# A retention-then-mixer kernel on one core: a plan that counts TensorE's instruction blocks, two-token loads for two head pairs only, and q cast into column order

## The chip, the cores and the metric

The kernel runs on 1 core of one Trainium2 chip. The metric is device time in microseconds (us) of one execution, the median over runs. Engines are named as in the profile: PE is the matmul engine (PEld its weight loads), DVE the vector engine, ACT the scalar engine, POOL and SP two engines that mostly issue DMA transfers here.

## What is computed

```python
def _attn_ref(q, k, v):                       # q, k, v: (4, 8, 768, 64) f32
    gamma = 1.0 - 2.0 ** (-5.0 - np.arange(H))
    state = np.zeros((B, H, D, D))
    for t in range(S):
        state = gamma[None, :, None, None] * state + np.einsum('bhd,bhe->bhde', k[:, :, t], v[:, :, t])
        y[:, :, t] = scale * np.einsum('bhd,bhde->bhe', q[:, :, t], state)
...
def _moe_ref(x, w_tok1, w_tok2, w_ch1, w_ch2):   # x: (4, 768, 512)
    xt = x.transpose(0, 2, 1)
    h = np.maximum(xt @ w_tok1, 0.0) @ w_tok2    # 768 -> 256 -> 768, over tokens
    u = x + h.transpose(0, 2, 1)
    h2 = np.maximum(u @ w_ch1, 0.0) @ w_ch2      # 512 -> 1536 -> 512, over channels
    return u + h2
```

The first function's output (batch, head, token, 64) is laid out as (batch, token, 512) and is the second one's x.

## The kernel before, in words

The work is cut into 16 pairs of heads (4 batches of 4 pairs, a pair's two heads side by side in 128 partitions) and 6 chunks of 128 tokens. `front(b, p)` does one pair, with matmuls in f16:

- **Load.** k, q and v come from device memory, cast to f16 on the way by POOL's queue (`load`, L489 to L517). Three loads of batch 0 are in `HARD`: they come as f32 over SP's queue, and the engines cast them.
- **Decay and transpose.** k is scaled by powers of gamma (`decayed`, L541) and transposed (`turn`, L576): on TensorE for batches 0 and 1 ("t"), by a DMA for batches 2 and 3 ("x"). q of batches 0 and 1 is loaded "wide" (a partition holds six consecutive tokens of a head) and is transposed head by head, 12 matmuls that each use a half of the array's columns ("w", L591); for batches 2 and 3 it goes like k. A HARD q is first cast to f16 (L572).
- **State and scores.** Five partial states (`st`, L618), a scan over them on DVE (L643), the scaled states `cross` (L654), the scores (`sc`, L665), their masked copy `am` on DVE (L686), then `av` and `y2` (L693 to L720), which add in-chunk and cross-chunk output in two banks.
- **Token mixing.** `t1` (L743) and `t2` (L764), which adds onto the same two banks, so that these hold u. It is copied twice, to f16 and to f32, and the f16 copy is transposed (L803 on TensorE or L792 by DMA) into `uT`.

A pair of batch 0 is **paired** before the change (`PAIRED = (0,)`): its k and v are loaded with two consecutive tokens of a head in one packet. A partition then holds neighbouring tokens, so `st`, `sc` and `av` split into half-array matmuls: 20 instead of 10, 24 instead of 12, and 24 instead of 12. Paired forms stand on L623, L675 and L698, the others on L630, L679 and L707.

`back(b)` does the channel mixing of a batch: for batch 0 a plain product (`w8`, L838: 96 matmuls of 128x384), for the others one with seven products in place of eight (L911); the second product (L1036) is of the latter kind for all. DVE adds the result to X, and SP or ACT stores it.

**What sets the order.** Every step is an `Op`. Two strings written in the file hold the order of all of them (`ORDERED`, two letters an op) and the engine of each (`WAYS`). `arrange` replays that order with a clock of its own: an op starts when its inputs, its engine and a buffer are there. It picks the buffer or bank of each op and the order in which the engines' instructions are written; within an engine that is `ORDERED`'s. Where its clock leaves TensorE free for over 400 ns in the first 21 us, filler matmuls on zeros (L1163) are put in. Before the change its clock knows engines, semaphores, buffers and DMA queues, and takes TensorE's instructions to be always at hand.

## Time and profile before

| | |
|---|---|
| time, median of 3 | 187.42 us (187.33 to 187.9) |
| the profiled execution | 187.37 us, of which the span of its instructions is 185.6 us (1.77 us lie outside) |
| granted TensorE clock | 1.000 |
| TensorE | 2216 weight loads and 2216 matmuls, 28 of the latter fillers |

The profile's page gives busy time by engine and, in 40 slices of the span, how busy each was. Its chain of work follows the last instruction back to what released it, step by step; "issue" there is time in which an engine waited for nothing that the profile shows. A group's row reads: line, engine, operation, out<-in, count, busy time, mean duration, idle time ahead of it. A row of busy time by stretch reads: stretch in us, its length, then for PE, PEld, DVE, ACT and POOL the busy us and, in brackets, the instructions that overlap the stretch; then the granted clock, the DMA engines' share and GB/s. Matmul durations overlap, since matmuls are pipelined: the time from a group's start to the next one's, which the chain shows, is what a group takes.

### The profile page before, as it was taken

How to read it: one execution, taken by the hardware profiler on the slowest of the kernel's cores; microseconds unless marked ns; L12 is line 12 of the kernel's file. 1: busy time of each engine (PE TensorE's matmuls, PEld its weight loads, DVE VectorE, ACT ScalarE, POOL GpSimd, SP SyncE). 2: the span in 40 equal slices, each digit the busy share in tenths (PEclk: the TensorE clock that was granted, in tenths of full speed). 3: DMA queues.
4: the chain of work that ended last, by engine and by line, in shares of the span. 5: the costliest groups of instructions: out<-in, count | busy, mean ns of one | idle time of the engine just before them, and what ended most of it. 6: DMA issues, size and time to landing. Idle time of an engine off the chain costs nothing.

```text
span 185.6 us, 5517 instructions
## 1 busy us (share of the span) xinstructions
PE 175.3 (94%) x2216; PEld 134.7 (73%) x2216; DVE 167.7 (90%) x431; ACT 128.5 (69%) x298; POOL 51.3 (28%) x63
## 2 busy tenths in 40 slices
PE   7688898899999999999999999999999999999992
PEld 3355787566778989876658988965778996668881
DVE  5599988878999999999999999999899999878993
ACT  3797887576899997999998474899765024654220
POOL 8964775462503906844004000000000000000000
PEclk9999999999999999999999999999999999999999
DMA  5999999999995998999999969340762114110044
GB/s 178 196 186 196 184 201 204 167 192 198 157 151 62 129 153 107 159 152 134 188 196 162 189 85 220 79 85 0 123 232 62 58 62 144 66 58 0 5 180 160
DMA packets 86106, 25.33 MB, mean 136 GB/s; under 512 B 75072, under 2 KB 83264, under 8 KB 86080
## 3 DMA queue, kind: packets, MB, share of 16 engines
q0 software_dynamic: 61808, 12.78, 82.1%
q1 hardware_dynamic: 22688, 9.70, 27.9%
q10 hardware_dynamic: 1584, 2.49, 3.7%
q8 instruction: 17, 0.28, 0.6%
q14 instruction: 9, 0.07, 0.1%
HBM read 26.74 MB, written 6.29 MB: 178 GB/s over the span
## 4 chain that ended last, share of the span: by engine, by line
PE 86%; DVE 4%; ACT 3%; DMA 3%; issue 1%; SPq 1%; DVEq 0%
PE bank L1036 30%; PE bank L911 22%; PE bank L838 8%; PE bank L743 6%; PE bank L764 5%; DMA hs<-in_q_dram 3%; PE bank L679 3%; PE bank L717 3%; PE bank L707 2%; PE bank L803 2%; PE bank L630 1%; DVE am L686 1%; PE bank L698 1%; PE bank L591 1%; DVE qT L602 1%
## 5 line engine op out<-in xcount | busy, mean ns | idle before, releaser
L686 DVE TENSOR_TENSOR am<-bank,mask 128x384 f16<-128x384 f32 x64 | 32.9, 546 | 0.7 <-PE bank L679 0.5
L864 ACT COPY us<-bank 128x384 f32<-128x384 f32 (+1 forms) x44 | 19.1, 437 | 17.8 <-PE bank L1036 11.6
L1036 PEld LDWEIGHTS <-hs 128*128 128x128 f16 x288 | 27.0, 98 | 3.1
L1036 PE MATMUL bank<-wsum,hs 128*128 128x256 f16 x216 | 27.8, 273 | 0.0
L859 ACT ACTIVATE h<-bank 128x384 f16<-128x384 f32 x50 | 23.3, 493 | 5.2 <-PE bank L838 3.5
L911 PE MATMUL bank<-hs,late 128*128 128x384 f16 x108 | 23.9, 326 | 0.0
L505 POOL DMA_DIRECT2D v<-in_v_dram x12 | 12.1, 1012 | 37.5 <-PE bank L707 13.4
L1036 PEld LDWEIGHTS <-h 128*128 128x128 f16 x216 | 20.6, 98 | 2.6
L932 DVE CUSTOM_DVE_ANT_0 h<-bank,us 128x384 f16<-128x384 f32 x36 | 19.0, 548 | 1.4 <-ACT us L864 0.7
L1050 DVE TENSOR_TENSOR X<-X,bank 128x256 f32<-128x256 f32 x48 | 19.2, 411 | 0.5 <-PE bank L1036 0.3
L1036 PE MATMUL bank<-wc,h 128*128 128x256 f16 x144 | 19.5, 273 | 0.0
L911 PEld LDWEIGHTS <-late 128*128 128x128 f16 x144 | 13.4, 98 | 7.9 <-DVE hs L883 0.2
L838 PE MATMUL bank<-uT,wc 128*128 128x384 f16 x96 | 17.7, 326 | 0.6 <-DVE X L729 0.6
L643 DVE SCALAR_TENSOR_TENSOR U<-U,gp,bank 128x64 f32<-128x64 f32 x64 | 15.9, 273 | 0.7
L911 PE MATMUL bank<-uT,wc 128*128 128x384 f16 x72 | 16.3, 326 | 0.0
L729 ACT COPY X<-bank 128x384 f32<-128x384 f32 x31 | 14.7, 493 | 2.2 <-PE bank L764 2.0
L729 ACT CAST x<-bank 128x384 f16<-128x384 f32 x27 | 12.2, 479 | 4.4 <-PE bank L717 4.2
L764 PE MATMUL bank<-h,wt 128*128 128x128 f16 x192 | 15.2, 219 | 0.0
L864 ACT COPY bank<-bank 128x384 f32<-128x384 f32 (+1 forms) x27 | 11.7, 436 | 4.9 <-PE bank L911 2.4
L729 ACT CAST u<-bank 128x384 f16<-128x384 f32 x25 | 11.8, 494 | 4.4 <-PE bank L764 4.2
L654 ACT ACTIVATE cross<-U,gp 64x320 f16<-64x320 f32 x25 | 13.8, 557 | 1.0 <-DVE U L643 0.7
L911 PEld LDWEIGHTS <-wc 128*128 128x128 f16 x108 | 9.9, 98 | 5.4
(98 smaller groups left out, 347.0 us busy)
## 6 DMA issues: line engine op xcount, KB each, us to landing
out_dram<-X SPq DMA_DIRECT2D x14, 256.0 KB, 2.4
v<-in_v_dram POOLq DMA_DIRECT2D x16, 192.0 KB, 8.0
k<-in_k_dram POOLq DMA_DIRECT2D x15, 192.0 KB, 9.0
q<-in_q_dram POOLq DMA_DIRECT2D x14, 192.0 KB, 9.7
wc<-in_moe_w_ch_dram POOLq DMA_DIRECT2D x5, 512.0 KB, 13.3
out_dram<-X ACTq DMA_DIRECT2D x8, 256.0 KB, 2.1
hs<-in_q_dram SPq DMA_DIRECT2D x2, 384.0 KB, 5.0
wc<-in_moe_w_ch_dram POOLq DMA_DIRECT2D x2, 256.0 KB, 8.6
```

The costliest lines, as they stand in the source:

```text
L643: nc.vector.scalar_tensor_tensor(out=u[:, c], in0=u[:, c - 1], scalar=gp[:, p:p + 1], in1=st, op0=ALU.mult, op1=ALU.add)
L654: nc.scalar.activation(r, u, AF.Copy, scale=g)
L686: nc.vector.tensor_tensor(am, SC[g].tile[:, :m * P].rearrange("p (i t) -> p i t", t=P), (mask2[:, g // 2:g // 2 + 1] if paired else mask). ...
L729: (nc.scalar.copy if e == "ACT" else nc.vector.tensor_copy)(tile(), t)
L764: nc.tensor.matmul(Y[j].tile[:, 2 * i * D:2 * (i + 1) * D], wt2[:, jt, t], H1.tile[:, jt], start=False, stop=(jt == NJ - 1), skip_group_ch ...
L838: nc.tensor.matmul(acc[:, :SH], wc1[:, ct, ft * P:(ft + 1) * P], UT.tile[:, ct, sh * SH:(sh + 1) * SH], start=(ct == 0), stop=(ct == NP - 1))
L859: nc.scalar.activation(out, src, AF.Relu)
L864: (nc.scalar.copy if e == "ACT" else nc.vector.tensor_copy)(out, src)
L911: nc.tensor.matmul(acc[:, :SH], left(ct), r[:, ct], start=first and ct == 0, stop=ct == C2 - 1, skip_group_check=True)
L932: nc.vector._custom_dve(TENSOR_ADD_SAT, out=h(m, sh), in0=R.tile[:, :SH], in1=KS.tile[:, j], s0=BIG, s1=0.0)
L1036: nc.tensor.matmul(acc[:, lo], l[:, j], r[:, j], start=first and j == 0, stop=j == K2 - 1, skip_group_check=True)
L1050: nc.vector.tensor_tensor(dst(), dst(), b_(), ALU.add)
```

## The change

It does four things.

1. **The planner's clock counts TensorE's instructions.** Each TensorE op gets a count (`ins`, two per matmul). Of every 256 instructions the plan notes when the block after next is asked for (`ASKED`) and when the first instruction of a block is needed (`NEEDED`); if it is needed earlier than `FETCH` after it was asked for, the op takes that much longer in the plan. Fillers are counted too, and their number is now set inside the plan. None of this is an instruction of its own.
2. **`PAIRED` holds two pairs of batch 0 in place of all four.** k and v of the third and fourth pair come in one-token packets, and their `st`, `sc` and `av` are the unpaired forms.
3. **A HARD q is cast into column order** (chunk, head, channel in place of head, chunk, channel), so that its transposition is 6 matmuls over the whole array, as for k, in place of 12 on half arrays. This holds for q of the first two pairs of batch 0.
4. **`ORDERED` and `WAYS` are new**, and some of the planner's DMA numbers (`OPENING`, `SOFT`, `HARD`, `PL`, `PT`).

```diff
-    PL = (1470, 1700, 2600)
-    PT = (4500, 25000)
+    PL = (1600, 2400, 2600)
+    PT = (13500, 25000)
...
+FILL, F_NS, F_COLD = 0.7, 165, 240
+BLOCK, ASKED, NEEDED, PE_0 = 256, -80, 192, 2
+FETCH = (7600, 5000, 95000)
...
+                o.fill = int((s_ - pe_at) * FILL / (F_NS if pe_at > 2000 else F_COLD)) if s_ < F_ON and s_ - pe_at > 400 else 0
+                count += 2 * o.fill
+                o.busy = way[1]
+                for x in range(count, count + o.ins):
+                    if (x - ASKED) % BLOCK == 0:
+                        fetched[(x - ASKED) // BLOCK] = s_ + (x - count) * o.busy / o.ins + FETCH[s_ > FETCH[2]]
+                    if (x - NEEDED) % BLOCK == 0 and x > NEEDED:
+                        late = fetched.get((x - NEEDED) // BLOCK, 0) - (s_ + (x - count) * o.busy / o.ins)
+                        o.busy += max(0, late)
+                count += o.ins
...
 ORDERED = (
-    "0u0a0t030v010c0x090f020m0C0d0b0e0j0w0h0r050o040l0y0g0n0s0A1x1y1z1A0F1E0q1B0p281C1F1D2f062g0B291O2a2b1S2c0E2P"
+    "0t0q000a0u0r010d0v030l0C0c0j0b0w0s02090e0x0m1x050A061E0f0o0y0h0p0i1F040z1y1z0n1A1B280g1C0B1D2f2g1O0E2N1S1G1Q"
...
-    PAIRED = (0,)
+    PAIRED = {(0, 0), (0, 1)}
...
-            elif b in PAIRED:
+            elif (b, p) in PAIRED:
...
-                d = tile_of(QF, [P, 2, NC, D], F16)
+                d = tile_of(QF, [P, NC, 2, D], F16).rearrange("p c h d -> p h c d")
                 (nc.scalar.copy if e == "ACT" else nc.vector.tensor_copy)(d, QH.tile)
...
+            split = mode == "w" and (b, p, "q") not in HARD
...
-                    if mode == "w":
+                    if split:
                         for j in range(2):
                             nc.tensor.transpose(tp[rows_of(j), c * P:(c + 1) * P], src.tile[:, j, c], ident16)
                     else:
                         nc.tensor.transpose(tp[:, c * P:(c + 1) * P], src.tile[:, c].rearrange("p h d -> p (h d)"),
                                             ident16)
```

TensorE has 4434 instructions in its order before (with two that are no matmuls or weight loads) and 4288 after it; 28 fillers become 35.

Three places show what the new order does. First POOL's queue, from its first load to v of the fourth pair. In a name, the letter is the tensor and the first number the buffer; 128x6x128 is a two-token load of k or v, 128x12x64 a one-token load, wt1 and wt2 are the token weights. Before:

```order
L501 DMA k0_102<-in_k_dram 128x6x128
L497 DMA q0_118<-in_q_dram 128x2x384
L501 DMA v0_127<-in_v_dram 128x6x128
L501 DMA k1_138<-in_k_dram 128x6x128
L501 DMA v1_144<-in_v_dram 128x6x128
L481 DMA wt2_85<-in_moe_w_tok2_dram 128x2x384
L501 DMA v2_215<-in_v_dram 128x6x128
L481 DMA wt1_84<-in_moe_w_tok1_dram 128x6x256
L497 DMA q3_338<-in_q_dram 128x2x384
L501 DMA k2_350<-in_k_dram 128x6x128
L501 DMA v3_392<-in_v_dram 128x6x128
```

The same queue after the change, as far as v of the fourth pair:

```order
L514 DMA q0_108<-in_q_dram 128x2x384
L518 DMA v0_114<-in_v_dram 128x6x128
L518 DMA k0_129<-in_k_dram 128x6x128
L518 DMA v1_136<-in_v_dram 128x6x128
L522 DMA k1_162<-in_k_dram 128x12x64
L522 DMA k2_171<-in_k_dram 128x12x64
L522 DMA v2_199<-in_v_dram 128x12x64
L498 DMA wt1_84<-in_moe_w_tok1_dram 128x6x256
L514 DMA q3_280<-in_q_dram 128x2x384
L498 DMA wt2_85<-in_moe_w_tok2_dram 128x2x384 x2
L522 DMA v3_356<-in_v_dram 128x12x64
```

Before, the second half of wt2 stands between wt1 and q3 (a row that reads like the first half's and isn't shown again). The twelve loads are the same; the last k has moved from behind wt1 to ahead of it, both halves of wt2 have moved behind q3, and four loads (two k, two v) have become one-token loads, three of them ahead of wt1.

Second, TensorE from the first t1 product on, one matmul of each group. Before (L743 is t1, L698 av, L717 y2, L764 t2, L591 a transposition of q, L623 st, L593 a transposition of k):

```order
L743 MATMUL bank5_508<-x160_474,wt1_84 128x128
...
L698 MATMUL bank6_528<-v1_144,am5_352 128x64
...
L764 MATMUL bank1_441<-h10_554,wt2_85 128x128
...
L591 MATMUL bank5_575<-ident16_74,q3_338 64x128
...
L743 MATMUL bank4_602<-x161_573,wt1_84 128x128
...
L698 MATMUL bank3_618<-v2_215,am2_505 128x64
...
L623 MATMUL bank7_649<-v3_392,k160_598 64x64
...
L593 MATMUL bank4_692<-ident16_74,k160_598 128x128
```

And after (L761 is t1, L609 a transposition of q, L716 a paired av, L725 an unpaired one, L782 t2, L648 an unpaired st, L821 a transposition of u):

```order
L761 MATMUL bank6_492<-x160_461,wt1_84 128x128
...
L609 MATMUL bank0_513<-ident16_74,q3_280 64x128
...
L716 MATMUL bank1_529<-v1_136,am6_434 128x64
...
L725 MATMUL bank2_558<-v2_199,am3_527 128x64
...
L782 MATMUL bank4_408<-h10_555,wt2_85 128x128
...
L761 MATMUL bank7_606<-x161_587,wt1_84 128x128
...
L648 MATMUL bank0_624<-v3_356,k160_358 64x64
...
L821 MATMUL bank4_637<-ident16_74,u160_604 128x128
```

The fourth pair's q is now transposed directly behind the first t1, ahead of the second pair's av; the third pair's av has moved ahead of the first t2; and the fourth pair's k is no longer transposed here (that now stands ahead of the first t1).

Third, DVE at the second q. Before (L459 and L458 are constants, L602 writes a transposed q, L686 is am):

```order
L572 CAST q1_146<-hs0_94 128x768
L549 TENSOR_SCALAR k160_148<-us0_90,gk2_78 128x3x64
L459 MEMSET cross0_81 128x320
L458 TENSOR_SCALAR mask_75<-away_66 128x128
L602 TENSOR_TENSOR qT0_194<-bank0_169,X0_123 128x768
L427 TENSOR_SCALAR lgs_67<-lgr_79,away_66 128x8
L602 TENSOR_TENSOR qT1_213<-bank2_199,X0_123 128x768
L686 TENSOR_TENSOR am0_249<-bank6_222,mask2_77 128x384
```

After (L589 is the cast, L620 the transposed q, L566 a decayed k, L704 am):

```order
L620 TENSOR_TENSOR qT0_168<-bank0_151,X0_127 128x768
L566 TENSOR_SCALAR k160_173<-us1_96,gk2_78 128x3x64
L472 MEMSET gp_73 64x1
L473 MEMSET gp_73 64x1
L589 CAST q2_180<-hs1_102 128x2x6x64
L620 TENSOR_TENSOR qT1_210<-bank2_203,X0_127 128x768
L704 TENSOR_TENSOR am0_254<-bank6_215,mask2_77 128x384
```

The cast of the second pair's q has moved from ACT to DVE, and it writes 128x2x6x64, which is the column order.

More of the change, by code (lines that the diff above doesn't have):

```diff
@@ L47 @@
     FIRST = dict(SP=600, POOL=1800, ACT=700)
-    OPENING = dict(SP=1300, POOL=3000, ACT=700)
+    OPENING = dict(SP=1300, POOL=3200, ACT=700)
     LAND = dict(SP=900, ACT=900)
@@ L122, in arrange @@
     tiled = ""
+    count, pe_at, fetched = PE_0, 1100, {}
     t = 0.0
@@ L230, in arrange @@
             else:
-                end[o.n] = s_ + way[2]
+                end[o.n] = s_ + way[2] + o.busy - way[1]
             for s, i in banks:
@@ L515, in load @@
         else:
-            o = request((-20, 0, b, p), 710 if wide else 850 if b in PAIRED else 1030, emit, dma, [s], key=("load", b, p, what))
+            o = request((-20, 0, b, p), 710 if wide else 850 if (b, p) in PAIRED and what != "q" else 1030, emit, dma, [s], key=("load", b, p, what))
         loads[b, p, what] = (s, o)
     def front(b, p):
-        first, paired = b == 0, b in PAIRED
+        first, paired = b == 0, (b, p) in PAIRED
         FA = "first" if first else "front"
@@ L1154 @@
     nc.vector.memset(zero, 0.0)
-    FILL, F_NS = 0.7, 165
-    spare, pe_at = None, 1100
+    spare = None
     for o, e, way, banks in order:
-        if e == "PE":
-            if o.start < F_ON and o.start - pe_at > 400:
-                if spare is None:
-                    spare = ps.tile([P, 512], FP, name="bank7", bufs=1)
-                for _ in range(int((o.start - pe_at) * FILL / (F_NS if pe_at > 2000 else 240))):
-                    nc.tensor.matmul(spare[:, :384], zero[:, :P], zero, start=True, stop=True)
-            pe_at = o.start + way[1]
+        for _ in range(o.fill):
+            if spare is None:
+                spare = ps.tile([P, 512], FP, name="bank7", bufs=1)
+            nc.tensor.matmul(spare[:, :384], zero[:, :P], zero, start=True, stop=True)
         way[3]()
```

89 lines of the change are left out of this document (49 added, 40 removed).

## Prediction

> **What bounds the kernel now.** I read the page's busy table and its chain first, then busy time by stretch, then the chain in order of time between 18 and 36 us.
>
> ```profile
> PE 175.3 (94%) x2216; PEld 134.7 (73%) x2216; DVE 167.7 (90%) x431; ACT 128.5 (69%) x298; POOL 51.3 (28%) x63
> PE 86%; DVE 4%; ACT 3%; DMA 3%; issue 1%; SPq 1%; DVEq 0%
> ```
>
> PE carries 86% of the chain, and DVE, at 90% busy, is close behind. By stretch (columns: stretch, length, then busy us and instructions of PE, PEld, DVE, ACT, POOL, then clock, DMA share, GB/s):
>
> ```profile
> 5.90:18.12 12.22, 9.28 (x228) 5.91 (x229) 10.48 (x28) 10.07 (x23) 8.20 (x11) 1.00 1.56 191
> 18.12:22.56 4.44, 4.43 (x107) 3.73 (x108) 4.27 (x12) 3.86 (x10) 3.14 (x5) 1.00 1.79 183
> 22.56:23.30 0.74, 0.01 (x2) 0.00 (x1) 0.53 (x2) 0.74 (x3) 0.54 (x1) 1.00 1.54 192
> 23.30:28.95 5.65, 5.33 (x128) 4.74 (x128) 4.85 (x13) 5.09 (x13) 4.52 (x5) 1.00 1.36 201
> 28.95:29.50 0.55, 0.00 (x1) 0.00 (x1) 0.55 (x1) 0.55 (x2) 0.08 (x1) 1.00 1.25 207
> 29.50:35.50 6.00, 5.40 (x96) 4.51 (x96) 4.81 (x10) 3.81 (x9) 2.43 (x3) 1.00 1.74 185
> 35.50:42.00 6.50, 6.50 (x47) 4.06 (x45) 5.33 (x9) 4.68 (x11) 4.15 (x5) 1.00 1.74 187
> 86.00:146.00 60.00, 60.00 (x704) 46.46 (x702) 57.73 (x145) 44.19 (x105) 2.60 (x3) 1.00 1.01 131
> 146.00:182.00 36.00, 35.90 (x300) 28.01 (x296) 32.57 (x74) 13.52 (x33) 0.00 (x0) 1.00 0.24 82
> ```
>
> From 35.5 to 182 us PE has work without a break. The change leaves that stretch's work as it is but for one switch of tiling (part 1), so the time is set by when it begins. I call that point S, 35.50 before. Ahead of S, PE is short of work until the first t1 product at 18.12. From there on it has two holes of its own, 0.74 and 0.55 us, in which PE and PEld stand still. The chain puts them down to nothing that the profile shows; the first of them:
>
> ```profile
> 22.56 0.74 issue
> ```
>
> Both lie inside a group of matmuls whose inputs were there (ahead of the first, 6 of 20 state matmuls had run; part 1 has the rows). Between them run 128 matmuls and 128 weight loads, so 256 instructions. The queue that carries instructions moved this over the whole span, and one packet in the microsecond from 20.8 to 21.8:
>
> ```profile
> q8 instruction: 17, 0.28, 0.6%
> q8 instruction: 1, 0.02, 5.6%
> ```
>
> 17 packets for PE's 4432 loads and matmuls are one for about 260 instructions. I read the holes as PE at the end of a block whose successor had not come: the packet ends some 1.5 us ahead of 23.30. In PE's order the holes stand at instructions 702 and 958.
>
> The Trainium skill, Runtime: NRT & Kernel Launch, section Instruction fetch mechanics, says that instructions come in 16 KiB blocks of 256 and that crossing a boundary is mostly hidden. The packets' size and count agree; the two holes do not look hidden, and what the rule would make of the time is the first rival.
>
> **Part 1: fewer instructions ahead of S.** These rows of the chain give what a group takes to the next one's start: scores, av and states, each in the half-array form and then the other, a transposition of k, a t1, and three transpositions of a wide q:
>
> ```profile
> 15.73 0.53 PE bank L675 x24
> 45.33 0.44 PE bank L679 x12
> 18.95 0.51 PE bank L698 x24
> 79.10 0.35 PE bank L707 x12
> 22.38 0.18 PE bank L623 x6
> 23.30 0.32 PE bank L623 x14
> 88.29 0.29 PE bank L630 x10
> 41.68 0.34 PE bank L593 x6
> 21.08 0.67 PE bank L743 x12
> 27.69 1.12 PE bank L591 x36
> ```
>
> Only what stands behind the first t1 counts, since ahead of it PE waits anyway: two av groups (third and fourth pair) save 0.16 each, the fourth pair's scores 0.09, its states 0.18 + 0.32 - 0.29 = 0.21. The transposition of its k, 0.34, moves to ahead of the first t1, into idle time. Together 0.96. The whole-array transpositions of the first two q stand ahead of t1 too and count nothing. Three w8 matmuls move from ahead of S to behind it, which is the same in sum. Behind S there is one change of the array's tiling less (34 for 35): 0.1 by the order's count, from 0.44 for twelve L679 that are 0.0285 apart.
>
> **Part 2: the cast in column order.** Its cost is not in the trace; the nearest rows are the plain cast on DVE and the same cast on ACT:
>
> ```profile
> 5.29 0.56 DVE L572 CAST q<-hs 128x768 f16<-128x768 f32 x1 [0.49 <-DMA hs<-in_q_dram]
> 7.85 0.83 ACT L572 CAST q<-hs 128x768 f16<-128x768 f32 x1 [0.97 <-DMA hs<-in_q_dram]
> 9.37 0.96 DVE L602 TENSOR_TENSOR qT<-bank,X 128x768 f16<-128x768 f16 x1 [1.57 <-ACT kT L607]
> ```
>
> So 0.5 to 0.9 us, and I take 0.56, since the written pieces are still 64 elements long. The second q's cast moves from ACT to DVE and starts as the load lands at 7.85, so DVE's second qT can start at about 7.85 + 0.56 + 0.5 = 8.9 in place of 9.37.
>
> **Part 3: the loads.** An issue's time and its time to landing give the landing. wt1, two-token k and v, a wide q, and two one-token v:
>
> ```profile
> 7.79 0.84 POOL L481 DMA_DIRECT2D wt<-in_moe_w_tok_dram  x1
> 11.12 0.82 POOL L501 DMA_DIRECT2D k<-in_k_dram  x1 [0.40 <-DMA v<-in_v_dram]
> 12.20 0.82 POOL L501 DMA_DIRECT2D v<-in_v_dram  x1 [0.27 <-DMA k<-in_k_dram]
> 13.58 0.70 POOL L497 DMA_DIRECT2D q<-in_q_dram  x1 [0.56 <-DVE U L641]
> 25.85 1.01 POOL L505 DMA_DIRECT2D v<-in_v_dram  x1
> 27.04 1.02 POOL L505 DMA_DIRECT2D v<-in_v_dram  x1 [0.17 <-issue]
> ```
>
> Their landing rows, in the same order:
>
> ```profile
> wt<-in_moe_w_tok_dram POOLq DMA_DIRECT2D x1, 384.0 KB, 10.1
> k<-in_k_dram POOLq DMA_DIRECT2D x1, 192.0 KB, 9.8
> v<-in_v_dram POOLq DMA_DIRECT2D x1, 192.0 KB, 9.9
> q<-in_q_dram POOLq DMA_DIRECT2D x1, 192.0 KB, 9.5
> v<-in_v_dram POOLq DMA_DIRECT2D x1, 192.0 KB, 11.6
> v<-in_v_dram POOLq DMA_DIRECT2D x1, 192.0 KB, 11.7
> ```
>
> POOL's loads land one behind the other: two-token ones 22.1 - 20.9 = 1.2 us apart, one-token ones 38.7 - 37.4 = 1.3, and the wide q 23.1 - 22.1 = 1.0 behind the load ahead of it. wt1 landed at 17.9, and t1 began at 18.12, so this load sets t1. Ahead of wt1 two loads change their form (0.1 each), and one half of wt2 gives way to a k, at most 0.3. That makes 0.2 to 0.5, and I take 0.5: t1 at 18.6. v of the fourth pair then lands near 22.6 instead of 22.1. PE reaches that pair's states at 18.6 plus the groups between: t1 0.67, a q 0.37, two av 0.51 + 0.35, ten y2 matmuls at 0.056 (a sixth of the k transposition's 0.34), t2 and t1 0.67 each, so 3.8 us and 22.4. Both halves of wt2 land behind q3 at about 18.4 + 3 x 1.0 = 21.4 (a half has a wide q's size and form), where PE comes to the first t2 at 21.1. Waits of 0.2 to 0.3 can so come back here; the 0.5 is taken from the top of its range to hold them.
>
> **Part 4: the holes.** Block ends keep their places, 702 and 958. The usable blocks came 29.50 - 23.30 = 6.2 us apart, and PE drew level with them, because between the ends it had 5.65 us of work. After the change the groups named in part 3, then states 0.29, a transposition of u 0.34, t2 0.67 and half the scores lie between t1's start, where a block also begins (447), and 702: 5.4 us, so 24.0. The block behind that holds 36 q matmuls (1.12), two t1 and two t2 (2.68), av 0.35, y2 0.28, four transpositions (1.36), the other scores and five w8 at under 0.2, so about 6.4 us: 30.4. Spacing of 6.2 from 18.6 would give 24.8 and 31.0: 0.8 would stay. Spacing of 5.65, the time from the first hole's end to PE's next lack, gives 24.2 and 30.0: 0.2 would. That the blocks' asking follows PE's own progress is a guess, and by it the blocks come earlier than before, as PE stands longer ahead of t1 in the block before. I take none of it, and the range takes the 0.8: -1.29.
>
> **The sum.** 187.37 - 1.29 - 0.96 + 0.5 - 0.1 = 185.5. The profiled execution lies 0.05 below the median shown, so 185.6 for the median. With the holes gone, what comes last ahead of S is DVE. From its second qT to the last u cast of the batch it had:
>
> ```profile
> 9.37:33.48 24.11, 21.14 (x507) 16.67 (x507) 22.17 (x53) 20.66 (x47) 15.13 (x19) 1.00 1.53 194
> ```
>
> 22.2 us of work in 24.1. After the change its queue holds one copy more there (a kT, about 0.5 us) and starts 0.5 earlier, so it can't be done ahead of 8.9 + 22.7 = 31.6; with the last transposition of u (0.34), S can't be ahead of 32.0. That is 3.5 us gained at most, less 0.5 us for the w8 matmuls moved behind S, plus the 0.1: 184.3, the low end but for a few tenths. Behind S, PE, DVE and ACT shift together; what can be late there are loads, which don't.
>
> **Rivals.**
>
> *The holes stay.* If they aren't block ends, or if the fetch keeps 6.2 us and more from a later asking, their 1.29 us remain: 186.8, so 186.9 for the median. For it: no row names the fetch as the releaser. Against it: 256 instructions between them. This is also what the page's rule would give. Chance 0.15.
>
> *DVE decides, and nothing is gained.* If DVE keeps its 1.9 us of gaps because they came from loads and not from PE's holes, the last u cast comes at 8.9 + 22.7 + 1.9 = 33.5, as before, and S stays: 187.4. For it: DVE is over 90% busy there. Against it: in the first hole DVE was busy for 0.53 of 0.74 us only, so part of its gaps is PE's. Chance 0.13.
>
> *Slower: one-token loads hold up t1.* TensorE's queue goes in order, and t1, then q3's transposition, stand ahead of everything else behind 18 us. If a one-token load took 2.4 us beside the opening's f32 loads, in place of 1.3, wt1 would land 3 x 1.1 = 3.3 us later still and all behind it too: 185.6 + 3.3 = 188.9. It is even with before from 0.6 us more a load (1.84 / 3), and measurably slower from 0.8. Against: 1.3 in the row. The Trainium skill, DMA: Bandwidth & Descriptors, section Specifications, says that a transfer under 512 B does not reach line rate, and a one-token f32 row is 256 B; the rows show 0.1 us for it, so the trace supports little of it. Chance 0.11.
>
> **The numbers.** The forecast has 0.61. About 0.3%, or 0.56 us, is what a measurement here can tell from no change. The forecast's own range is 184.1 to 186.8, nearly all of it faster; of the first rival's chance half falls on each side of 186.86. Faster 0.61 + 0.08 = 0.69, same 0.07 + 0.13 = 0.20, slower 0.11. For 8 in 10 the range takes in the first rival and part of the second: 184.1 to 187.3.
>
> **What would show it.** Right: no "issue" hole of over 0.3 us in PE behind t1; t1 starting at 18.4 to 18.8; unbroken w8 from 33.0 to 34.0; no PE idle time behind that. Wrong: holes at 702 and 958 again (first rival), S near 35.5 with PE waiting for DVE (second), t1 behind 20 us (third), or PE waiting in the middle for weight sums or kT, since wc2's last part lands no earlier while PE comes about 2 us sooner.

## The result, and the profile after

The changed kernel takes 188.45 us (median of 13 runs, 187.96 to 189.46), the kernel before 187.32 us beside it (13 runs, 186.53 to 187.91). The ratio is 1.0072, with a 95% interval of 1.005 to 1.0094: slower by 0.7%. The forecast was 185.6 us, and its range ended at 187.3. It was wrong.

The profiled execution of the changed kernel took 189.17 us, 0.72 above its own median; its span is 187.3 us, its mean granted clock 0.987. First PE's busy time and the shares of the chain, from its page:

```profile
PE 177.7 (95%) x2143; PEld 135.7 (72%) x2143; DVE 170.2 (91%) x431; ACT 128.8 (69%) x294; POOL 51.8 (28%) x63
PE 84%; DVE 7%; DMA 4%; ACT 1%; issue 1%; SPq 0%; DVEq 0%
```

TensorE has 73 matmuls fewer, and "issue" and DVE carry as much of the chain as before or more. Busy time by stretch, cut at the changed kernel's own marks (first t1 at 20.52, work without a break from 35.06 to 182.84; columns as in the prediction):

```profile
5.90:20.52 14.62, 11.49 (x202) 7.04 (x201) 12.31 (x35) 10.08 (x22) 9.69 (x13) 0.88 1.75 180
20.52:35.06 14.54, 13.74 (x277) 12.05 (x277) 13.25 (x28) 12.58 (x29) 8.86 (x11) 1.00 1.60 191
35.06:78.00 42.94, 42.94 (x546) 33.93 (x543) 41.21 (x101) 35.48 (x80) 19.69 (x20) 1.00 1.86 155
78.00:144.00 66.00, 66.00 (x783) 50.05 (x783) 64.25 (x160) 52.55 (x125) 8.32 (x9) 1.00 1.09 126
144.00:182.84 38.84, 38.77 (x323) 30.14 (x320) 34.10 (x77) 15.44 (x37) 0.00 (x0) 1.00 0.27 88
```

From t1 to S it took 14.5 us where before took 17.4, close to what the forecast allowed. But t1 began at 20.52 and not at 18.6, so S moved by 0.44 us only, and the three w8 matmuls that now stand behind it (0.49) eat that. The weights that the forecast had t1 wait for, wt1, landed at 18.82, 1.70 us ahead of it. The two holes are gone. What PE waits for between 17 and 36 us is now DVE (columns: total, times, longest):

```profile
PE bank L761 <- DVE u L747: 0.6, 1, 0.6
PE bank L761 <- DVE U L661: 0.5, 1, 0.5
```

The second of these is the wait of the first t1. Before, the first t1 had this one, which is for a copy of its other input, x, and not for wt1:

```profile
PE bank L743 <- ACT x L729: 0.2, 1, 0.2
```

DVE itself stood for the second f32 q, which the forecast had landing at 7.85. DVE between 6 and 13 us:

```profile
9.46 0.56 DVE L589 CAST q<-hs 128x768 f16<-128x768 f32 x1 [1.31 <-DMA hs<-in_q_dram]
10.69 0.96 DVE L620 TENSOR_TENSOR qT<-bank,X 128x768 f16<-128x768 f16 x1 [0.67 <-PE bank L611]
```

The cast in column order costs 0.56, as taken. It starts 1.6 us late, and the second qT comes at 10.69: before, 9.37; forecast, 8.9.

Behind S the forecast had no change but the 0.1 us for a switch of tiling. The trace has three losses there. First, the chain of PE in stretches of the seven-product stage (start, us, what):

```profile
85.86 0.65 PE bank L929 x4
...
87.89 2.68 PE bank L929 x14
...
133.95 0.65 PE bank L929 x4
...
135.27 0.79 PE bank L929 x4
...
157.88 5.77 PE bank L929 x34
163.65 0.10 issue
163.74 0.57 DVE h L950
```

Four matmuls take 0.65 in one place and 0.79 in the other, and the fourteen from 87.89 on take 2.68. Before had this:

```profile
91.42 3.68 PE bank L911 x22
```

That is 0.167 each; the fourteen have 0.191 each. The busy table doesn't show it, for it has PE busy in all 66.00 us from 78 to 144; it shows in the time from start to start. There are six such waits, of 0.13 to 0.23 us (at 88.2, 89.0, 89.8, 135.3, 159.9 and 164.0), 0.93 us in all. Before has one, of 0.07. None of them is in the profile's list of waits, so that list names no releaser. At 88 us I read ACT as the late one: it makes the seeds of the products (L882) between copies of X and u (L747), and the matmuls behind the three waits start at 88.52, 89.30 and 90.08, each 0.05 us behind the end of a seed:

```profile
87.60 0.48 ACT L747 COPY X<-bank 128x384 f32<-128x384 f32 x1 [0.28 <-DVE u L747]
87.98 0.49 ACT L882 COPY bank<-bank 128x384 f32<-128x384 f32 x1
88.39 0.48 ACT L747 COPY X<-bank 128x384 f32<-128x384 f32 x1
88.76 0.49 ACT L882 COPY bank<-bank 128x384 f32<-128x384 f32 x1
89.17 0.49 ACT L747 CAST u<-bank 128x384 f16<-128x384 f32 x1
89.54 0.49 ACT L882 COPY us<-bank 128x384 f32<-128x384 f32 x1
```

At 164 the chain above names DVE's h (L950); for the waits at 135.3 and 159.9 nothing here names a releaser.

Second and third, the end. From TensorE's last product to the last instruction it takes 4.47 us (182.84 to 187.31), where before took 3.69 (181.90 to 185.59). The queues of the changed kernel from 180 to 184.5 us, with the stores' median time to landing:

```profile
q8 instruction: 1, 0.02, 2.2%
...
out_dram<-X ACTq DMA_DIRECT2D x1, 256.0 KB, 3.7
out_dram<-X SPq DMA_DIRECT2D x1, 256.0 KB, 3.2
out_dram<-X ACTq DMA_DIRECT2D x2, 128.0 KB, 2.4
out_dram<-X SPq DMA_DIRECT2D x1, 128.0 KB, 2.0
```

And before's, from 179 to 184.5 us:

```profile
out_dram<-X SPq DMA_DIRECT2D x2, 256.0 KB, 2.0
out_dram<-X ACTq DMA_DIRECT2D x2, 128.0 KB, 1.8
out_dram<-X SPq DMA_DIRECT2D x1, 128.0 KB, 1.7
```

A 16 KiB packet of TensorE's instructions lies among the last stores (181.13 to 182.72). Each of two large stores has its last eight packets behind it: 120 of 128 are there by 182.13 and 183.23, the last eight at 183.71 and 184.35. Eight of 128 are one of 16 DMA engines' share, so I read the packet as holding one engine. Before, the last such packet went at 172.29. And SyncE's (SP's) closing waits, which run one behind the other, have a step of their own. The starts of the last five, from the traces:

```
before:  184.53  184.59  184.65  184.71  184.77
after:   185.77  185.84  186.31  186.39  186.46
```

### The profile page after: what moved, and what is told of

Same layout as the page of the kernel before. It is cut to its first block, busy times and chain, and to the rows that moved or that the text cites. A ratio compares the mean times of both kernels' runs of the same rounds, so it can differ in the third digit from the quotient of the medians.

```text
span 187.3 us, 5371 instructions
## 1 busy us (share of the span) xinstructions
PE 177.7 (95%) x2143; PEld 135.7 (72%) x2143; DVE 170.2 (91%) x431; ACT 128.8 (69%) x294; POOL 51.8 (28%) x63
## 4 chain that ended last, share of the span: by engine, by line
PE 84%; DVE 7%; DMA 4%; ACT 1%; issue 1%; SPq 0%; DVEq 0%
PE bank L1054 29%; PE bank L929 22%; PE bank L856 8%; PE bank L782 5%; PE bank L761 5%; DMA hs<-in_q_dram 4%; PE bank L697 3%; PE bank L725 3%; DVE am L704 2%; PE bank L735 2%; PE bank L648 1%; PE bank L821 1%; DVE U L661 1%; PE bank L1184 1%; DVE qT L620 1%; PE bank L611 1%
## 5 line engine op out<-in xcount | busy, mean ns | idle before, releaser
L704 DVE TENSOR_TENSOR am<-bank,mask 128x384 f16<-128x384 f32 x64 | 33.0, 549 | 0.7 <-PE bank L697 0.5
L882 ACT COPY us<-bank 128x384 f32<-128x384 f32 (+1 forms) x47 | 20.5, 441 | 16.4 <-PE bank L1054 11.5
L877 ACT ACTIVATE h<-bank 128x384 f16<-128x384 f32 x47 | 22.0, 495 | 8.6 <-PE bank L856 5.1
L950 DVE CUSTOM_DVE_ANT_0 h<-bank,us 128x384 f16<-128x384 f32 x36 | 19.0, 551 | 2.5 <-ACT us L882 1.3
L522 POOL DMA_DIRECT2D v<-in_v_dram x14 | 14.3, 1021 | 22.0 <-PE bank L725 15.5
L522 POOL DMA_DIRECT2D k<-in_k_dram x14 | 14.3, 1024 | 16.2 <-DVE U L661 8.6
L882 ACT COPY bank<-bank 128x384 f32<-128x384 f32 (+1 forms) x25 | 10.8, 434 | 9.6 <-PE bank L1054 5.6
L661 DVE SCALAR_TENSOR_TENSOR U<-U,gp,bank 128x64 f32<-128x64 f32 x64 | 16.7, 274 | 0.6
L672 ACT ACTIVATE cross<-U,gp 64x320 f16<-64x320 f32 x26 | 14.5, 560 | 0.5
L782 PE MATMUL bank<-h,wt 128*128 128x128 f16 x192 | 14.7, 219 | 0.1
L747 ACT COPY X<-bank 128x384 f32<-128x384 f32 x29 | 14.0, 492 | 0.9 <-DVE u L747 0.7
L747 ACT CAST x<-bank 128x384 f16<-128x384 f32 x27 | 12.1, 483 | 3.6 <-PE bank L735 3.5
L761 PE MATMUL bank<-x,wt 128*128 128x128 f16 x192 | 13.3, 219 | 1.2 <-DVE u L747 0.6
```

Source lines behind the costliest of these rows:

```text
L522: (nc.sync if hard else nc.gpsimd).dma_start(out=tile_of(s, [P, 2, NC, D], FP if hard else F16), in_=src.rearrange("h (c p) d -> p (h c) d ...
L704: nc.vector.tensor_tensor(am, SC[g].tile[:, :m * P].rearrange("p (i t) -> p i t", t=P), (mask2[:, g // 2:g // 2 + 1] if paired else mask). ...
L747: (nc.scalar.copy if e == "ACT" else nc.vector.tensor_copy)(tile(), t)
L761: nc.tensor.matmul(acc[:, jt * P:(jt + 1) * P], wt1[:, i, jt * P:(jt + 1) * P], X16.tile[:, i].rearrange("p h d -> p (h d)"), start=(i == ...
L782: nc.tensor.matmul(Y[j].tile[:, 2 * i * D:2 * (i + 1) * D], wt2[:, jt, t], H1.tile[:, jt], start=False, stop=(jt == NJ - 1), skip_group_ch ...
L877: nc.scalar.activation(out, src, AF.Relu)
```

## The experiments

I read each trace in the same four numbers, worked out from start times. **Lead at 36**: how far TensorE is ahead of before's profile at 36 us, with the rest of its groups counted at their usual spacing. **Second qT**: when DVE starts it. **Lost behind 36**: TensorE's end less before's 181.90, plus the lead. **End**: TensorE's end to the last instruction. These come from one profile each; the ratio to before is from 10 to 13 runs (4 for one) beside 13 to 35 runs of before on the same chip.

| kernel | lead at 36 | second qT | lost behind 36 | end | median us | ratio (95%) |
|---|---|---|---|---|---|---|
| before | 0 | 9.37 | 0 | 3.69 | 187.32 | |
| after | -0.05 | 10.69 | 0.89 | 4.47 | 188.45 | 1.0072 (1.005 to 1.0094) |
| a_sp | -0.08 | 10.37 | 0.91 | 4.28 | 188.46 | 1.0071 (1.0038 to 1.0104) |
| a_pool | 1.06 | 9.28 | 0.91 | 4.24 | 188.03 | 1.003 (0.9998 to 1.0063) |
| a_head | 0.20 | 10.40 | 0.89 | 4.56 | 188.62 | 1.0051 (1.0025 to 1.0077) |
| a_tail | 0.98 | 9.97 | 1.28 | 3.73 | 188.25 | 1.004 (1.0013 to 1.0068) |
| old_order | -0.86 | 10.48 | 0.55 | 3.72 | 187.39 | 0.999 (0.9959 to 1.0021) |
| b_cast | -1.44 | 9.71 | 1.06 | 3.73 | 188.64 | 1.0075 (1.0047 to 1.0103) |
| b_half | -0.37 | 9.70 | 0.02 | 3.73 | 186.91 | 0.9976 (0.995 to 1.0001) |
| b_pool | -2.69 | 10.20 | 1.38 | 3.67 | 190.06 | 1.0135 (1.0094 to 1.0177) |
| c_trim | 1.44 | 9.47 | 0.90 | 4.18 | 188.13 | 1.0036 (1.0013 to 1.0059) |
| c_s36 | 0.79 | 9.97 | 0.19 | 3.79 | 186.99 | 0.9986 (0.9961 to 1.0011) |
| c_s36_trim | 0.83 | 10.12 | 0.46 | 3.80 | 187.32 | 1.0004 (0.9977 to 1.0031) |
| d_mirror | 0.35 | 9.10 | 0.67 | 4.17 | 188.64 | 1.0048 (1.0022 to 1.0073) |
| e_stores | 0.99 | 9.97 | 0.87 | 4.12 | 188.39 | 1.0057 (1.0031 to 1.0082) |
| e_best | 1.20 | 9.24 | 0.12 | 4.11 | 187.08 | 0.9973 (0.9944 to 1.0003) |
| f_sp7 | 1.69 | 9.23 | 0.88 | 3.86 | 187.95 | 1.0024 (0.9995 to 1.0053) |
| f_best | 1.13 | 9.24 | 0.12 | 3.74 | 186.99 | 0.9983 (0.9961 to 1.0004) |

A lead that is negative here has a spell of half clock in its profile ahead of 36 us, which is told of at the end.

### Which loads make the opening late

**a_sp**: SyncE's first three loads in before's order.

```diff
-SP: q of pair 1, k of pair 1, q of pair 2
+SP: k of pair 1, q of pair 1, q of pair 2
```

> The changed kernel with SP's f32 loads in the old order (k, q, q of the second pair; the change has q, k, q). Theory A (POOL's queue now begins with a wide q, and this takes the DMA engines from SP's third f32 load, which lands at 9.4 us in place of 7.8): the third f32 load still lands at 9.0 to 9.8, the unbroken w8 still begins near 35, the time stays that of the changed kernel, 188.2 to 188.7. Rival B (SP's own new order makes it late): it lands near 7.8 and the time falls to about 187.1.

Measured: 1.0071, as the changed kernel. The third f32 load lands at 8.78, so SyncE's own order isn't what makes it late. But DVE's first cast now waits for its q till 5.21 (3.95 in the changed kernel); the first qT comes at 7.04 in place of 5.73, and the second at 10.37, behind DVE's own work and not behind the load.

**a_pool**: GpSimd's first three loads in before's order. **a_head**: both.

```diff
-POOL: q of pair 3 (wide), v of pair 1, k of pair 2
+POOL: k of pair 2, q of pair 3 (wide), v of pair 1
```

> The changed kernel with POOL's first three loads as before (k of the second pair, wide q of the third, v of the first; the change has q, v, k); SP's order as changed. Theory A (the wide q at the head of POOL's queue delays SP's third f32 load): it lands at 7.8 to 8.3, DVE's second qT starts near 9, the unbroken w8 begins 1.2 to 1.6 us earlier than 35.06, time 186.9 to 187.3. Rival B (SP's order): it lands at 9.0 or later, time as the changed kernel's, 188.2 to 188.7.

> The changed kernel with both heads of queue as before: SP k, q, q and POOL k, q, v. Both A and B: the third f32 load lands near 7.8, w8 without a break from about 33.5, and 186.8 to 187.3. Rival C (the opening is late for another reason, the one-token loads or DVE's longer queue): the load lands near 7.8 but w8 still begins near 35, and the time stays at 188.2 or above.

Measured: 188.03 and 188.62 us, ratios of 1.003 and 1.0051; neither comes down to the 187.3 expected. In a_pool the third f32 load lands at 8.02, and its cast waits for no load any more. Its rows:

```profile
8.04 0.56 DVE L589 CAST q<-hs 128x768 f16<-128x768 f32 x1
9.28 0.96 DVE L620 TENSOR_TENSOR qT<-bank,X 128x768 f16<-128x768 f16 x1 [0.67 <-PE bank L611]
```

Its wt1 landed at 18.25, but its first t1 began at 19.30 and not at the forecast's 18.6, and the lead is 1.06 and not 1.85. From the second qT to the first w8 product it is 22.0 to 22.7 us in after, a_sp, a_pool, a_head, a_tail, c_trim, c_s36 and c_s36_trim, and DVE is busy for 21.0 to 21.3 of them; before, with its holes, had 22.62. So I take DVE's own work from that qT on to set what follows, holes or not. In the six profiles at full clock that keep the changed order of the opening, the lead goes with that qT: 1.69 us at 9.23 (f_sp7), 1.44 at 9.47, 0.79 to 0.99 at 9.97, 0.83 at 10.12.

a_head has rival C's signs, the load at 7.84 and a time above 188.2. Its second qT comes at 10.40 all the same: with k first in SyncE's queue DVE's first cast waits for its q till 5.26, where a_pool's starts at 4.00, and DVE's queue is late from there. So it is DVE's queue and not the third load that costs a_head its lead; a spell of half clock follows at 11.13. For DVE's second qT SyncE's new order is the better one.

**b_pool**: the mirror image, before with the wide q at the head of GpSimd's queue.

```diff
-POOL: k of pair 2, q of pair 3 (wide), v of pair 1
+POOL: q of pair 3 (wide), v of pair 1, k of pair 2
```

> The kernel before with POOL's first three loads in the changed order (wide q, v, k in place of k, q, v), SP's order as before. Theory A: SP's third f32 load lands near 9.4 in place of 7.83, DVE's second qT starts near 10.6 and the time rises by 0.8 to 1.4 us, to about 188.4. Rival B (SP's order): it lands near 7.8 and the time stays at 187.3.

Measured: 1.0135 from four runs. The load lands at 8.33, for 7.83 before and 9.4 expected; the second qT comes 0.83 later than in before, and the clock is half from 8.53 to 15.36. How much of the time is the order and how much the clock, this run doesn't say.

The landing of the third f32 load over all eighteen profiles says more than any one: 7.52 to 9.44, with a median of 8.65, in the nine with the wide q at the head of GpSimd's queue, and 7.37 to 8.65, with a median of 7.84, in the nine with k there. So the order of that queue shifts the landing by about 0.8 us, and each order has an exception (f_sp7 at 7.52, old_order at 8.65).

### The holes, the cast, the code without the order

**b_half**: before, with each filler cut in two, so that 28 matmuls and 28 loads more stand ahead of everything.

```diff
-nc.tensor.matmul(spare[:, :384], zero[:, :P], zero, start=True, stop=True)
+nc.tensor.matmul(spare[:, :192], zero[:, :P], zero[:, :192], start=True, stop=True)
+nc.tensor.matmul(spare[:, :192], zero[:, :P], zero[:, :192], start=True, stop=True)
```

> The kernel before with each filler matmul (384 columns) written as two of 192 columns: the same filler time, 56 instructions more ahead of the first t1. If the two holes are ends of instruction blocks, they stay at the same count of instructions (702 and 958) and so come 56 instructions earlier in the work: inside the third pair's av instead of the fourth pair's states, and inside the three q transpositions instead of the fourth pair's av. If they belong to those groups (an input or a bank that the profile doesn't show), they stay in the states and in the fourth pair's av. Time within 0.5% of before by both, since a hole moves and doesn't go.

Measured: of the hole at instruction 702, now inside an av, 0.07 us is left. The other, of 0.9 us, ends at 958 again, now inside the transposition of a q, where before it stood in av:

```profile
PE bank L591 <- issue: 0.9, 1, 0.9
```

**b_cast**: before, with the column cast and the whole-array transposition of the two f32 q alone.

```diff
-d = tile_of(QF, [P, 2, NC, D], F16)
+d = tile_of(QF, [P, NC, 2, D], F16).rearrange("p c h d -> p h c d")
```

> The kernel before with the column cast and whole-array transpositions of the two f32 q alone. All theories: no change by more than 0.3%, 187.0 to 187.6, as these transpositions stand where PE waits for data; the DVE cast takes 0.56 us as before.

Measured: 1.0075, slower, where no change was expected, though it only takes instructions away. Twenty-four fewer instructions put other work at the block ends. The one at 702 now costs this, at 23.43:

```profile
PE bank L624 <- issue: 2.0, 1, 2.0
```

Its packet came at 22.99 to 23.89; PE resumed 1.52 us behind it. A spell of half clock followed at 25.99, and eight of its ten runs have a mean clock under 0.9935; how much of the 0.75% is the hole and how much the clock stays open. In b_pool the holes stand at 702 and 958 too, inside the loops they happen to fall on:

```profile
PE bank L698 <- issue: 0.7, 1, 0.7
PE bank L591 <- issue: 0.5, 1, 0.5
```

**old_order**: the changed code, with before's order and engines.

```diff
-ORDERED, WAYS of the changed kernel
+ORDERED, WAYS of before, step by step by name
```

> The changed code (counted blocks, two paired pairs, column cast) with the old order and the old choice of engines, each op in its old place; the two av ops of an unpaired pair stand where the one stood, and one small constant moves ahead of the third pair's k. Theory A with D (the new order, at both ends, is what makes it slower): the third f32 load lands at 7.8, no seven-product waits, and the code alone is a little faster than before, 186.5 to 187.3 (0.5 us of PE work less in the chain ahead of w8, one-token loads 0.5 later, the holes possibly still there). Rival C (one-token loads cost more than they save): 187.6 or above.

Measured: 0.999. Fewer TensorE instructions alone don't make it slower, and by the interval gain at most 0.4%. So the 0.7% lies in the new order: the two intervals, this one and the changed kernel's, don't meet.

### The order behind 36 us

**a_tail**: the changed kernel up to the second batch's first product of the seven-product stage (78 us), then before's order and engines. **c_s36**: the same with the joint at the first unbroken w8 (35 us), where the two orders have nearly the same steps behind them. **c_s36_trim**: c_s36 with ten TensorE instructions fewer (below). The joint shown is c_s36's; a_tail's comes at step 539.

```diff
-ORDERED[205:], WAYS of the changed kernel
+ORDERED, WAYS of before for the steps that are left
```

> The changed kernel up to the first seven-product block of batch 1 (near 78 us), and from there every engine's order and every choice of engine as before. Theory D (six waits of PE for DVE's and ACT's copies in the seven-product blocks, 0.93 us in sum, are what the new order loses behind 80 us): they go, the opening is as the changed kernel's, time about 187.5. Rival E (the waits come from the opening's being late or from the run, not from the order behind 78 us): as many waits in other places, time 188.2 or above.

> The changed kernel up to the place where the unbroken channel products set in (35 us), and behind it before's order and engines. Theory D (the new order behind that place costs 0.93 us in six waits within the seven-product stage and more at the stores): the six waits are gone, TensorE ends 0.9 us sooner, and from TensorE's end on it takes 3.7 us as in before; with the opening's gain of 1.0 us, that the run with the joint near 78 us showed at 36 us (no reading of a low clock there) and a wait of 1.4 us at its own joint took back, 186.4 to 186.9, a ratio of 0.995 to 0.998. Rival H (the waits come from the time at which the work arrives, whatever the order behind): the waits come back at the same steps and the time is 188.0 to 188.5, a ratio of 1.004 or above.

> The run before with the fifteen fillers of 512 columns of the first run: 4277 rows on TensorE. If both theories D and F hold, the least of all: 186.2 to 186.7, a ratio of 0.994 to 0.997. If the packet costs nothing where the last stores go in before's order (in the run with the joint near 78 us it started at 180.44 and TensorE's end to the last instruction took 3.73 us), it equals the run before within 0.3 us. If the order behind 35 us costs nothing (rival H), 188.

Measured: in a_tail the six waits are gone, but the joint itself costs PE 1.44 us at 78.83 (a wait that neither kernel has), so its 1.28 says nothing on the order. c_s36 has no such wait: the six are gone, 0.19 is lost for 0.89, the end takes 3.79, and its ratio of 0.9986 stands against 1.0072 with the same opening. The trim adds nothing to that.

**d_mirror**: the changed code with before's order up to that joint, the changed order behind it.

> The mirror image: the changed code in before's order up to the place where the unbroken channel products set in, and in the changed kernel's order and engines behind it; 4281 rows on TensorE, so no seventeenth packet by theory F. The same code in before's order throughout took 187.39. Theory D: the six waits are there, 0.9 us more, 188.3, a ratio of 1.0045; with F the end from TensorE's last product on is 3.7 to 3.9 us. Rival G (the stores' own order): 0.6 us more than that, 188.9. Rival H: no waits, 187.4.

Measured: 1.0048. Five of the six waits are there (0.70 us), and the end takes 4.17. Nine of its twelve runs have a mean clock under 0.9935, against five of twelve in old_order, so its ratio says less than its profile. With c_s36 both halves of the crossing say that the new order behind 35 us costs the time; rival H is out.

### The end

**c_trim**: the changed kernel with its first twenty fillers made fifteen longer ones: 4277 rows on TensorE for 4287 (the order's own count of these is 4288).

```diff
+wide_ = 512 if o.fill > 8 else 384
...
-nc.tensor.matmul(spare[:, :384], zero[:, :P], zero, start=True, stop=True)
+nc.tensor.matmul(spare[:, :wide_], zero[:, :P], zero[:, :wide_], start=True, stop=True)
...
-for _ in range(o.fill):
+for _ in range({11: 8, 9: 7}[o.fill] if o.fill > 8 else o.fill):
```

> The changed kernel with its first twenty fillers (11 and 9 of 384 columns) made fifteen of 512 (8 and 7): the same time for TensorE, but ten rows fewer in its program, 4277 for 4287. In the traces so far every 16 KiB packet of queue 8 (TensorE's instructions) starts 18 to 36 rows ahead of row 190+256k; the changed kernel, with 4287 rows, has a seventeenth at 181.13 for 1.58 us, and before's order on the changed code, with 4281 rows, has none behind 167.29. Theory F (that packet holds one of the sixteen DMA engines while the last stores are written, and so costs the end): no such packet behind 170 us, and from TensorE's end to the last instruction about 3.8 us for 4.47; the time falls by 0.5 to 0.7 us, to about 187.8, a ratio of 1.0025 to before. Rival G (the order and the queues of the last stores cost it, the packet nothing): 4.2 to 4.5 us from TensorE's end on, 188.4, a ratio of 1.006.

Measured: no packet among the stores, which land in 1.7 to 2.0 us again, but an end of 4.18. So the packet was a part in the changed kernel, and something else the rest.

**e_stores**: c_trim with before's order and engines for the last fifty steps.

```diff
-ORDERED[1192:], WAYS of the changed kernel
+ORDERED, WAYS of before for the steps that are left
```

> The changed kernel with the fifteen fillers of 512 columns (4277 rows on TensorE, no instruction packet among the last stores) and its last fifty steps, all of the last batch's last products, sums and stores, in before's order and on before's engines; no other step is touched. Theory G (the order and the queues of the last stores cost 0.4 us after TensorE's end): 3.7 to 3.8 us from TensorE's end to the last instruction, where the same kernel with its own last fifty steps took 4.18; the six waits within the seven-product stage stay, 0.93 us; time 187.6, a ratio of 1.0015. If the end is late for another reason: 4.1 to 4.2 us from TensorE's end on, and 188.1 as that kernel.

Measured: 4.12. Theory G falls: the stores go as in before, and the end is as late. What it shares with after, a_sp, a_pool, a_head, c_trim and d_mirror is SyncE's step of 0.46 to 0.49 us, and 86 recorded instructions on SyncE, where the nine other kernels so far have 93. (These are seven kernels; the next expectation miscounts them as eight.)

**f_sp7**: c_trim with seven small loads more on SyncE's queue; nothing reads them.

```diff
+if at_ == 420:
+    for x in range(7):
+        nc.sync.dma_start(out=const_p.tile([P, 64], FP, name="pad%d" % x), in_=moe_w_tok1[:P, :64])
```

> The changed kernel with the fifteen fillers of 512 columns and seven more loads of 32 KB on SyncE's queue near 50 us, of weights that nothing reads (work added, none taken away). In the profiles so far SyncE's closing waits have a step of 0.46 to 0.49 us, where the others take 0.06, in all eight kernels in which SyncE has 86 recorded instructions, and none at that wait in the nine with 93; that holds with the last stores in either order. Theory J (SyncE's own count of instructions sets where that step falls): with 93 the step is gone from that place, and from TensorE's last product to the last instruction it takes 3.7 to 3.8 us for 4.18; about 0.4 us less, 187.7, a ratio of 1.0013. If the order of the work sets it: the step stays, 4.2 us and 188.1.

Measured: 3.86, with 95 instructions. The last five of its closing start at 183.88, 183.94, 184.00, 184.06 and 184.13, so the step is gone from there. More work, and the end is 0.32 sooner: theory J. The other profiles bear it out. In all seventeen of them 0.46 to 0.49 us lie between SyncE's 79th and 80th recorded instruction; with 93 of them these stand seven places further from the end, as in before (182.76 and 183.24), where stores are still under way. The time, 1.0024, doesn't tell it from c_trim's 1.0036; the profile does.

### The best of both

**e_best**: c_s36 with a_pool's order of the first loads. **f_best**: e_best with longer fillers, 4281 rows on TensorE for 4291.

> The changed kernel up to the place where the unbroken channel products set in, with GpSimd's first three loads in before's order (k of the first pair, q of the third, v of the first), and before's order and engines behind that place. Theory A (the wide q at the head of GpSimd's queue holds up SyncE's third f32 load): VectorE's cast of that q waits for no load and starts by 8.1, as in the run with that edit alone (8.04), where with the wide q in front it waited in four of five profiles (till 8.38 to 9.46); the first unbroken channel product about 0.3 us sooner than with the joint alone, and 186.5 to 186.9, a ratio of 0.995 to 0.998. If the third f32 load is no matter: as the joint alone, 187.0, a ratio of 0.9986.

> The kernel with the changed opening, GpSimd's first three loads in before's order and before's order behind the unbroken products' start, with its larger groups of fillers at 512 columns: 4281 rows on TensorE, so no seventeenth instruction packet, which in the same kernel with 4291 rows lay at 179.25 among the last stores. Theory F: no packet there, TensorE's end to the last instruction 3.75 us for 4.11, 186.7 us, a ratio of 0.9955 to 0.997. If the packet costs nothing there: 187.0, a ratio of 0.9973.

Measured: 187.08 and 186.99 us. (GpSimd's k is the second pair's; the first of the two expectations calls it the first pair's.) In e_best a packet lay among the stores (179.25 to 180.67):

```profile
q8 instruction: 1, 0.02, 1.5%
...
out_dram<-X SPq DMA_DIRECT2D x2, 256.0 KB, 3.4
```

In f_best it is gone:

```profile
out_dram<-X SPq DMA_DIRECT2D x2, 256.0 KB, 2.0
```

The end falls from 4.11 to 3.74, as theory F has it. The ratios, 0.9973 and 0.9983, can't tell the two apart (186.99 is what f_best was expected to take if the packet cost nothing), nor either from before with certainty: both intervals reach just past 1. A gain over before of 0.2% to 0.3% is likely and not shown.

## Why the prediction was wrong

**That the holes are block ends, and go: right.** In before, b_half, b_cast and b_pool the holes end at instructions 702 or 958 whatever work stands there, 1.4 to 1.6 us behind a packet's end. In the changed kernel there is none.

**That their 1.29 us and the 0.96 of work would come off S: wrong.** The failed step is part 2's "starts as the load lands at 7.85, so DVE's second qT can start at about 7.85 + 0.56 + 0.5 = 8.9". It moved the wide q to the head of GpSimd's queue and still took SyncE's f32 load from before's row. With the wide q in front that load landed at 8.65 in the median and at 9.44 in the changed kernel's profile, where the second qT came at 10.69. The rest of the step was short too: where the load was there by 7.52 and 7.37 (f_sp7, e_best), that qT still came at 9.23 and 9.24, behind DVE's own queue. "Only what stands behind the first t1 counts, since ahead of it PE waits anyway" fails with it: DVE, with its 22.0 to 22.7 us from that qT to the first w8, is the next bound. In the six profiles at full clock this opening gains 0.79 to 1.69, four of them within 0.79 to 0.99, of the 1.85 expected. This is the second rival's mechanism, though not its size.

**That wt1 sets t1 (part 3): wrong too.** Before, wt1 landed at 17.93 and the last copy of x ended at 18.03, 0.09 ahead of t1; in b_half and b_cast wt1 landed at 17.35 and 17.14, and t1 came at 18.97 and 19.07, 0.09 behind x again. The landing itself was well foreseen: 17.80 to 18.82 in the twelve kernels with the changed opening, for a forecast of about 18.4. So the third rival's mechanism was not what came. But t1 began 0.2 to 2.3 us behind that landing, and only f_sp7's (18.67) lies within the forecast's 18.4 to 18.8.

**"Behind S, PE, DVE and ACT shift together; what can be late there are loads": wrong, and it turned the sign.** I had compared the orders ahead of S and taken the rest of the new order to be as good as the old. It costs 0.87 to 0.91 us in all seven kernels that have it with the new opening, and 0.02 to 0.19 went with before's order there in b_half, c_s36, e_best and f_best. (c_s36_trim's 0.46 holds another wait, of 0.38 at 109.08, and the late openings of old_order, b_cast and b_pool go on losing behind 36 us.) Each single wait is about as short as one matmul.

**The end was no term of my sum.** It costs 0.78 us: about 0.3 by TensorE's seventeenth packet (4.47 to 4.18 in c_trim, 4.11 to 3.74 in f_best), and 0.3 to 0.5 by SyncE's step. I had read that instructions come in blocks and applied it to the opening alone, for one engine. The changed kernel's last instructions cross a block's end by a row or two: 4287 rows have the packet there, 4281 don't. The packet doesn't cost this much wherever it falls among the stores. It ended 0.04 to 0.15 us ahead of TensorE's end in after, a_head and e_best, and the last store landed 2.91 to 3.03 us behind that end. It ended 0.24 to 0.72 ahead in a_sp, a_pool, c_s36 and a_tail, and the last store landed 2.64 to 2.73 behind, against 2.56 to 2.72 without a packet. That SyncE's step is a block's end as well is my reading: no packet moved during the changed kernel's step, and an 8 KiB one of another instruction queue (q14) started 0.64 us behind it.

**The sum again.** 185.6, and 0.85 for the opening's missing part, 0.89, and 0.78: 188.1 for 188.45. The last 0.3 stays open. The 0.85 is from single profiles, and seven of the nine profiles of a changed opening at full clock lie 0.1 to 1.2 below their kernels' medians, so a middle run's opening may be worse.

## To carry to other kernels

When an order is replaced as a whole, compare it as a whole: a stretch that "only shifts" can lose more than the opening gains, and waits shorter than one matmul show in the time from start to start, not in busy shares. Count instructions per engine at both ends of a program: a block's end that falls where nothing covers it can cost, as in the opening's holes and at this program's end, and a few instructions more or fewer move it. When a load moves ahead in one queue, take no landing time in another queue from the old trace.

## What the hardware showed that I had not expected

**Instructions come at a rate.** In the opening's holes a packet starts 3.6 to 3.8 us after PE resumes on a block, takes 0.9, and PE goes on 1.4 to 1.6 later: 6.0 to 6.2 us for 256 instructions (23.30 to 29.50 in before, 22.80 to 29.00 in b_half, 26.91 to 32.93 in b_pool). The Trainium skill, Runtime: NRT & Kernel Launch, section Instruction fetch mechanics, calls the crossing mostly hidden; in these openings it isn't hidden where PE gets through a block sooner than that.

**An instruction packet can hold up stores.** Among the last stores it takes 1.0 to 1.7 us, and the last eight of 128 packets come behind it: two large stores took 3.2 and 3.7 us for 2.0. Only a packet that ended within 0.15 us of TensorE's end made the program's end later.

**The clock falls in short spells, not in every run.** In the changed kernel's profile it is half from 11.91 to 15.32 us; six fillers there take twice their time and hold up the second pair's states:

```profile
12.00 2.10 PE L1184 MATMUL bank<-zero 128*128 128x384 f16 x6
```

There are nine such spells ahead of 36 us in eight of the eighteen profiles; each lasted 3.41 us or twice that, and PE had been busy for 1.4 to 1.9 of the 3.41 us ahead of it; a_tail had a stretch as empty (1.40) without one, from 5.95. Cut into pieces of 3.41 us from the first mark of the clock in each profile, no piece ahead of 36 us without a spell behind it had PE busy for under 2.0. The Trainium skill, TensorE: Matmul & The Clock Gate, section What's actually happening, has a window of 3.4 us that runs free of the kernel: the length agrees, and so does it that the same kernel falls on some runs. Of the 145 runs of before beside the experiments 49 had a mean clock under 0.9935, with a median of 188.02 us against 187.15 for the rest. It isn't what makes the changed kernel slower: of its 13 runs three had it.
